# A gated recurrence followed by a SwiGLU layer on one core: integer additions moved to VectorE, gate products put ahead of the angles, loads and rows put in another order

## The chip, the cores and the metric

The kernel runs on one core of a Trainium2 chip. A core has engines that each work through their own queue of instructions in order: TensorE (PE in the profile; its weight loads are PEld), VectorE (DVE), ScalarE (ACT), GpSimd (POOL) and SyncE (SP), which here only issues DMA transfers. Engines wait for each other through semaphores. The metric is the device time of one execution in microseconds (us). Times shown are medians of several runs; the profile is of one execution.

## The reference

Two blocks follow each other. The first is a recurrence over 768 time steps for 4 x 8 heads of width 48, with a complex decay per step and feature:

```python
mag = np.sqrt(a_re * a_re + a_im * a_im)
scale = np.minimum(mag, 0.999) / (mag + 1e-06)
a_re_n, a_im_n = (a_re * scale, a_im * scale)
for t in range(S):
    new_re = ar * S_re - ai * S_im
    new_im = ar * S_im + ai * S_re
    S_re, S_im = (new_re + k v^T, new_im)
    y[t] = q[t] @ S_re
```

The second takes the 3072 rows of 384 features that come out, normalises each by its root mean square, and computes `(silu(xn @ w_gate) * (xn @ w_val)) @ w_out` with 1536 hidden features. The three weights arrive as 64-bit floats and are narrowed to 32 bits on the chip.

## The kernel before, in words

**Tiling.** The 3072 rows are 24 chunks of 128. Gates are worked out in 13 units: units 0 and 1 are one chunk each, units 2 to 12 two chunks each, so chunk 2n and 2n+1 belong to unit n+1 from chunk 2 on. Two chunks make a group of the second block (g0 to g11).

**Gates** (`gates`, L772 to L850). From re and im of a unit come, on ScalarE and VectorE in turn: the magnitude by way of reciprocal roots, cut off at 0.999; its running product p along time by a scan (L807); the angle by an arctangent (L798); its running sum by a scan (L816), reduced to a fraction of a turn (L823 and after), then a sine and a cosine (L836, L838). k is multiplied by a refined reciprocal of p, q by p, and four products with sine and cosine, ks, k, qs and q, are the "rotated" rows. ScalarE's functions lie in tables: a change of function can need a load of 1.28 us (ACT_TABLE_LOAD). A unit's first step (L772) overwrites a tile that the rotation of the unit before it reads.

**Moving rows** (`move_rows`, L861). A DMA brings the rotated rows into the tiles kr and qr, 96 partitions deep, in three transfers for each of the four. Units 0 and 1 send ks and k on SP's queue and qs and q on POOL's; the others all four on SP's. The final products `ends` go out to DRAM (dec, L873) and come back in another shape (decay, L876); SP waits for dec before it issues decay.

**Chunks.** TensorE computes for each chunk the scores s (L1014), which VectorE masks (am, L1019); it transposes k (kt, L1035), which ScalarE copies (L1039); it forms the chunk's contribution to the state (L1057); and y from both (L1087). Then come sums of squares (ss, L1110), their mean on DVE (L1115), a root on POOL (L1120), its spreading (L1123), a copy rb on ScalarE (L1128) and xT on VectorE (L615).

**Second block.** For each group, twelve gv tiles (L1160), each twelve matmul passes with a piece of w_gate and of w_val; silu on ScalarE (L1164), a product on VectorE; then four output halves (L1184), each over half of the hidden features. Three PSUM buffers hold gv tiles and outputs.

**Weights** (`fetch`, `narrow`). There are 18 pieces: 0 to 11 alternate w_gate and w_val, 12 to 17 are w_out. A raw piece of 768 KB is fetched; ScalarE turns its low words into a fraction (share, L956); VectorE shifts the high words (L961) and adds the sign (L615); GpSimd adds the two as integers (L968). The first six pieces (EARLY) are issued on POOL's queue from the start, the others on SP's after unit 0's rows. Raw buffers are shared: a later piece waits until an earlier one is narrowed.

**What sets the order.** A planner written out in Python (`Order`) holds a list of lanes, each a sequence of steps with an engine, an assumed length and needs. It repeatedly takes the step that can begin first, with an added "late" per lane, and emits its instructions, so its assumed times fix the order in each engine's queue; the actual waits come from the data. `RATE` is its assumed transfer rate, and `holds` tells it that a GpSimd addition keeps VectorE busy. `busy` (L644) emits matmuls without use, as many as fill the gap that the planner expects on TensorE, 9 us at most.

The lines that carry the rest:

```python
for i, (o, x, f) in enumerate((("ks", "k", s), ("k", "k", y), ("qs", "q", s), ("q", "q", y))):
queue = nc.gpsimd if u < 2 and i > 1 else nc.sync
nc.gpsimd.tensor_tensor(out=to, in0=part["t"], in1=to, op=ALU.add)
[("re", 0) if aside else ("moved3", 0), ("piece", before) if before is not None else None],
```

## Time and profile before

| | |
|---|---|
| median of four runs | 831.5 us (826.74 to 837.05) |
| profiled execution, whole | 829.65 us |
| its span from first to last instruction | 827.5 us |
| PE busy | 761.2 us, 92% |
| DVE busy | 430.2 us, 52% |
| ACT busy | 360.8 us, 44%; 69 table loads of 1.28 us |
| POOL busy | 79.6 us, 10% |
| granted TensorE clock, mean | 0.948 |
| TensorE matmuls without use | 28.7 us (L644) |

In the page, engine rows of 40 digits show the busy share of 40 equal slices in tenths; PEclk is the TensorE clock that the chip granted, in tenths of full speed. A row of the timeline gives start, duration, engine, line, operation, output<-inputs, shapes and a count, and in brackets the idle time before it with what ended it. A row of the waits gives who waited for whom, the total, how often, and the longest. A row of the chain gives start, duration and what the time went to, followed back from the last instruction to end; "SPq" is SyncE's queue, "DMA a<-b" a transfer in flight.

### The profile page before, as it was taken

What the parts mean: (1) busy time and instruction counts of PE and PEld (TensorE: products, weight loads), DVE (VectorE), ACT (ScalarE), POOL (GpSimd) and SP (SyncE); (2) the same over time, 40 slices, a digit from 0 to 9 for tenths busy, and PEclk for the clock granted to TensorE, in tenths of its full rate; (3) what the DMA queues carried; (4) which work ended last, traced back from release to release, by engine and by line L of the source; (5) the groups of instructions that cost most, each with busy time, mean ns of one, the idle gap of its engine ahead of it and who ended that gap; (6) DMA issues with size and microseconds to landing.
All of it is one profiled execution on the core that took longest, in us unless ns stands there. A gap on an engine that the chain in (4) does not pass through costs nothing.

```text
span 827.5 us, 12028 instructions
## 1 busy us (share of the span) xinstructions
PE 761.2 (92%) x4820; PEld 608.2 (73%) x4820; DVE 430.2 (52%) x709; ACT 360.8 (44%) x565; POOL 79.6 (10%) x103
## 2 busy tenths in 40 slices
PE   5078967989998999999999999999999999999996
PEld 2066835778886878988678888678888778886783
DVE  4666999857675775857784766122211213320220
ACT  6542475657675767767664775101111101110110
POOL 6344432200000000000010000000000000000000
PEclk9556979989998999999999999999999999999999
DMA  8929537562747267554635470046100106200510
GB/s 199 198 62 241 141 114 128 120 117 43 114 88 130 45 113 121 120 77 97 78 112 75 122 115 1 10 97 143 40 0 1 58 17 192 79 1 28 179 61 23
DMA packets 100975, 76.48 MB, mean 92 GB/s; under 512 B 39664, under 2 KB 89584, under 8 KB 100912
## 3 DMA queue, kind: packets, MB, share of 16 engines
q1 hardware_dynamic: 98128, 69.74, 39.7%
q0 software_dynamic: 1920, 5.51, 3.1%
q8 instruction: 40, 0.66, 0.4%
q10 hardware_dynamic: 864, 0.39, 0.2%
q14 instruction: 23, 0.19, 0.1%
HBM read 51.98 MB, written 4.76 MB: 69 GB/s over the span
## 4 chain that ended last, share of the span: by engine, by line
PE 74%; DMA 9%; DVE 7%; SPq 4%; ACT 2%; issue 2%; POOL 0%; DVEq 0%; ACTq 0%
PE gv_ps L1160 38%; PE out_ps L1184 20%; PE s_ps L1014 6%; PE y_ps L1087 4%; PE state_ps L1057 3%; SPq L861 3%; DMA q<-in_q_dram 3%; DMA dec<-ends 2%; PE ss_ps L1110 1%; PE kt_ps L1035 1%; DMA qr<-q 1%; DMA qr<-qs 1%; DMA vz<-in_v_dram 1%; DVE re L816 1%; DMA hT<-in_w_val_dram 1%
## 5 line engine op out<-in xcount | busy, mean ns | idle before, releaser
L1160 PE MATMUL gv_ps<-xT,wg 128*128 128x256 f32 x864 | 213.7, 384 | 0.4 <-DVE xT L615 0.3
L1160 PE MATMUL gv_ps<-xT,wv 128*128 128x256 f32 x864 | 210.3, 379 | 0.0
L1184 PE MATMUL out_ps<-wo,hT 128*128 128x384 f32 x576 | 196.6, 494 | 7.8 <-POOL wo L968 7.8
L1160 PEld LDWEIGHTS gv_ps<-xT,wg 128*128 128x128 f32 x864 | 163.2, 192 | 26.6 <-DVE xT L615 2.3
L1160 PEld LDWEIGHTS gv_ps<-xT,wv 128*128 128x128 f32 x864 | 164.6, 190 | 22.5
L1184 PEld LDWEIGHTS out_ps<-wo,hT 128*128 128x128 f32 x576 | 108.0, 192 | 76.6 <-POOL wo L968 9.6
L612 DVE TENSOR_TENSOR hT<-gv_ps,hT 128x256 f32<-128x256 f32 x144 | 59.7, 421 | 189.6 <-ACT hT L1164 189.2
L1164 ACT ACTIVATE hT<-gv_ps 128x256 f32<-128x256 f32 x144 | 54.1, 383 | 211.2 <-PE gv_ps L1160 210.7
L1014 PE MATMUL s_ps<-qr,kr 96*128 96x128 f32 x384 | 56.5, 308 | 43.2 <-DMA kr<-k 30.5
L1014 PEld LDWEIGHTS s_ps<-qr,kr 96*128 96x128 f32 x384 | 52.5, 219 | 47.3 <-issue 47.3
L1120 POOL TENSOR_TENSOR rs<-ssq,mhalf 128x1 f32<-128x1 f32 x24 | 18.5, 771 | 580.1 <-DVE ssq L1115 580.1
L1193 ACT COPY ot<-out_ps 128x384 f32<-128x384 f32 x24 | 11.5, 480 | 63.8 <-PE out_ps L1184 63.8
L615 DVE SCALAR_TENSOR_TENSOR xT<-y_ps,gcol,rb 128x128 f32<-128x128 f32 x72 | 20.8, 345 | 35.5 <-ACT rb L1128 29.6
L1019 DVE TENSOR_TENSOR am<-s_ps,causal 128x512 f32<-128x512 f32 x48 | 32.1, 684 | 11.8 <-PE s_ps L1014 11.2
L1057 PEld LDWEIGHTS state_ps<-vz,kt 128*96 128x96 f32 x320 | 31.9, 175 | 1.6 <-issue 0.5
L1164 ACT ACT_TABLE_LOAD x25 | 32.1, 1283 | 0.4
L1128 ACT COPY rb<-ss_ps 128x128 f32<-128x128 f32 x24 | 6.4, 265 | 59.4 <-PE ss_ps L1123 59.4
L1057 PE MATMUL state_ps<-vz,kt 128*96 128x48 f32 x320 | 31.9, 256 | 0.0
L1039 ACT COPY kt<-kt_ps 128x384 f32<-128x384 f32 x40 | 17.2, 478 | 25.2 <-PE kt_ps L1035 25.2
L1087 PE MATMUL y_ps<-am,vz 128*32 128x128 f32 x768 | 27.6, 287 | 0.0
L990 DVE TENSOR_REDUCE least__113<-raw 128x1 f32<-128x768 f32 x18 | 17.0, 945 | 19.3 <-DMA raw<-in_w_out_dram 16.0
L1110 PEld LDWEIGHTS ss_ps<-ones,sq 128*128 128x128 f32 x144 | 19.7, 197 | 8.5 <-ACT sq L1105 5.0
(113 smaller groups left out, 819.6 us busy)
## 6 DMA issues: line engine op xcount, KB each, us to landing
raw<-in_w_out_dram SPq DMA_DIRECT2D x12, 768.0 KB, 4.4
k<-in_k_dram SPq DMA_DIRECT2D x24, 192.0 KB, 3.1
q<-in_q_dram SPq DMA_DIRECT2D x24, 192.0 KB, 4.0
vz<-in_v_dram SPq DMA_DIRECT2D x24, 192.0 KB, 4.6
out_dram<-ot SPq DMA_DIRECT2D x24, 192.0 KB, 2.0
raw<-in_w_gate_dram SPq DMA_DIRECT2D x6, 768.0 KB, 4.6
raw<-in_w_val_dram SPq DMA_DIRECT2D x6, 768.0 KB, 4.5
re<-in_a_re_dram SPq DMA_DIRECT2D x33, 128.0 KB, 2.8
```

The costliest lines, as they stand in the source:

```text
L612: nc.vector.tensor_tensor(out=o, in0=x, in1=y, op=op)
L615: nc.vector.scalar_tensor_tensor(out=o, in0=x, scalar=c, in1=y, op0=op0, op1=op1, **kw)
L861: queue.dma_start(out=two[name][rows + j * L:rows + (j + 1) * L], in_=t[("ks", "k", "qs", "q")[i]][:, j])
L1014: nc.tensor.matmul(u["s_ps"][a][:, h], lhsT=u["k"][:, a * HH + h], rhs=u["q"][:, a * HH + h], start=True, stop=True)
L1019: nc.vector.tensor_tensor(out=u["am"][a], in0=u["s_ps"][a], op=ALU.mult, in1=causal.unsqueeze(1).to_broadcast([C, HH, C]))
L1057: nc.tensor.matmul(u["st_ps"][:, h], lhsT=u["kt"][h // HH][:, h % HH], rhs=u["v"][:, h, 0:D], start=True, stop=True)
L1087: nc.tensor.matmul(u["y_ps"][32 * p:32 * (p + 1), j], lhsT=columns(left, j, odd, p), rhs=right(h), start=side == 0 and i == 0, stop=side = ...
L1110: nc.tensor.matmul(u["ss_ps"][:, 0:1], lhsT=u["sq"][:, d], rhs=ones, start=d == 0, stop=d == ND - 1)
L1120: nc.gpsimd.tensor_tensor(out=u["rs"], in0=u["ssq"], in1=mhalf, op=ALU.pow)
L1160: nc.tensor.matmul(ps[:, i], lhsT=w_[:, f * P // FW, d, cols], rhs=t["xT"][:, d], start=d == 0, stop=d == ND - 1)
L1164: nc.scalar.activation(out=t["hT"][:, f], in_=t["gv", f][:, 0], func=AF.Silu)
L1184: nc.tensor.matmul(t["o_ps", i], lhsT=t["hT"][:, f, i * C:(i + 1) * C], rhs=wo[:, f], start=f == 0, stop=f == NF - 1)
```

## The change

It does the following, all in the fast path:

- The integer addition at the end of narrowing goes from GpSimd to VectorE; `holds` is dropped.
- In `gates`, the running product, the reciprocal root of p and the products of k and q come ahead of the angle; the range check (relu with an accumulator) comes early; the four rotations come in the order ks, qs, k, q.
- `move_rows` takes the rows in that order, so for units 0 and 1 transfers alternate between SP's and POOL's queue.
- v of unit 0 is loaded along with unit 1's; unit 2's gates are loaded after unit 1's q.
- EARLY is 3 instead of 6. Ahead of these pieces POOL copies one column of unit 1's k, so that they begin once that has landed. The other pieces start after unit 1's rows.
- w_out pieces may be narrowed later (WO); the planner's rate is 0.22 for all queues together.
- The matmuls without use ahead of chunk 0's scores are seven that read unit 0's ks.

```diff
-    RATE = 0.2
+    RATE = 0.22
...
-            for n in range(first_, first_ + m):
+            for n in range(0 if u == 1 else first_, first_ + m) if u else ():
...
-                more["late"] = lambda: 0.1 if ("piece", 11) in order.ends else 0.6
+                more["late"] = lambda: 0.1 if ("piece", 11) in order.ends else 0.3
...
+            check = E("ACT", 0.2 + ac_us(n1), [], lambda: act_(out=qs, in_=qs, func=AF.Relu, bias=width,
+                                                               accum_out=range_[:, u:u + 1]), K("checked"))
...
-            yield E("DVE", tt_us(n1), [K("y0")], lambda: tt(im, im, y), K("t0"))
...
-            yield E("DVE", tt_us(n1), [K("abs")], lambda: tt(re, re, y))
...
             yield E("DVE", 0.4 + n1 / 480, [], products, K("p"))
 
+            yield E("DVE", tt_us(n1), [K("y0")], lambda: tt(im, im, y), K("t0"))
+            yield E("DVE", tt_us(n1), [K("abs")], lambda: tt(re, re, y))
+            yield E("DVE", tt_us(n1), [], lambda: stt(im, re, 2.0, im, ALU.subtract, reverse0=True), K("tan"))
+            yield E("ACT", ac_us(n1), [K("p")], lambda: act_(out=r, in_=p, func=AF.Abs_reciprocal_sqrt),
+                    table=["ars"])
+            yield E("ACT", ac_us(n1), [], lambda: act_(out=r, in_=r, func=AF.Square), K("r2"))
+            yield E("ACT", ac_us(n1), [K("tan")], lambda: act_(out=im, in_=im, func=AF.Arctan), table=["atan"])
+            yield E("ACT", ac_us(n1), [], lambda: act_(out=im, in_=im, func=AF.Copy, scale=0.5 / PI), K("turns"))
+            yield E("DVE", tt_us(n1), [K("r2")], lambda: tt(ks, p, r))
+            yield E("DVE", tt_us(n1), [], lambda: stt(r, ks, 2.0, r, ALU.subtract, reverse0=True))
+            yield E("DVE", tt_us(n1), [K("k")], lambda t=t: tt(t["k"], t["k"], t["r"]))
+            yield E("DVE", tt_us(n1), [K("q")], lambda t=t: tt(t["q"], t["q"], t["p"]))
...
-            for i, (o, x, f) in enumerate((("ks", "k", s), ("k", "k", y), ("qs", "q", s), ("q", "q", y))):
+            for i, (o, x, f) in enumerate((("ks", "k", s), ("qs", "q", s), ("k", "k", y), ("q", "q", y))):
...
-                queue = nc.gpsimd if u < 2 and i > 1 else nc.sync
+                queue = nc.gpsimd if u < ASIDE and i % 2 else nc.sync
...
-    EARLY = 6
+    EARLY = 3
...
+        yield step("POOL", 0.2, [("k", 1)],
+                   lambda: nc.gpsimd.tensor_copy(out=behind, in_=UN[1]["k"][:, 0, 0:1]), ends=["rows in"])
...
-                       [("re", 0) if aside else ("moved3", 0), ("piece", before) if before is not None else None],
+                       ["rows in" if aside else ("moved1", 1), ("piece", before) if before is not None else None],
...
             def total(to=to.bitcast(I32), part=part):
-                nc.gpsimd.tensor_tensor(out=to, in0=part["t"], in1=to, op=ALU.add)
+                tt(to, part["t"], to, ALU.add)
...
-            yield step("POOL", 2.3, [("both", i)], total, ends=[("piece", i)], holds=("DVE", 1.2))
+            yield step("DVE", tt_us(n), [], total, ends=[("piece", i)], **more)
...
-                    if a == 0:
+                    if a == 0 and n:
                         busy(flat(u["s_ps"][a]))
+                    elif a == 0:
+                        rotated = flat(UN[0]["ks"])
+                        for _ in range(7):
+                            nc.tensor.matmul(flat(u["s_ps"][a])[:, 0:ND * C], lhsT=ident, rhs=rotated,
+                                             start=True, stop=True)
```

## The prediction

> **What bounds the kernel now.** I read the page's busy table and slices first, then the chain that ended last, then the waits, then the timeline of the first 270 us.
>
> ```profile
> PE 761.2 (92%) x4820; PEld 608.2 (73%) x4820; DVE 430.2 (52%) x709; ACT 360.8 (44%) x565; POOL 79.6 (10%) x103
> PE   5078967989998999999999999999999999999996
> PEclk9556979989998999999999999999999999999999
> ...
> PE s_ps L1014 <- DMA kr<-k: 30.5, 2, 29.9
> ...
> 17.53 20.71 DMA q<-in_q_dram
> 38.26 6.37 DMA dec<-ends
> ...
> 131.73 5.65 DMA dec<-ends
> ...
> 168.65 6.88 DMA qr<-q
> ...
> 251.71 7.48 DMA dec<-ends
> 259.27 3.75 PE s_ps L1014 x16
> ```
>
> TensorE bounds the whole from slice 12 on. What can be won lies in the first third: slices 1 to 12, where it waits or runs at a low clock (5, 5, 6 and 7 tenths in slices 1, 2, 3 and 5; each is 20.7 us).
>
> To add up such a stretch I use a **lag**: clock time minus the full-speed TensorE work that stands ahead in its queue. Full-speed prices are from chain rows that run warm: scores of a chunk 1.85 us, turned keys 0.7, state 1.32, each half of y 0.95, ss 0.85, a gv tile (12 matmuls) 2.59, half an output row block 3.88. The whole kernel is 706.2. The first scores of chunks 0, 2, 4, 6, 8 and 10 start at 44.2, 137.5, 175.7, 221.5, 259.3 and 302.8 with 0, 47.3, 79.9, 119.6, 152.6 and 193.0 ahead. The lags are 44.2, 90.2, 95.8, 101.9, 106.7 and 109.8. TensorE's last output matmul ends at 820.5: lag 114.3. So 110 of 114 us are lost by chunk 10, and only that stretch can pay. 7.0 us of closing work follow, the same in both.
>
> **Part by part.** I take the changed kernel's built order of instructions on each engine and put durations of this trace on it.
>
> Start to the first scores. Before, six weight pieces go out on POOL's queue from 5.5 us, and unit 1's k row, issued at 12.25, reaches its consumer at 36.1 (23.8 us at the longest). Changed, k, q and v of unit 1 stand on SP ahead of unit 2's gates (issue done by about 8.8 by the same 0.6 us rows; unit 2's gates, 2 us later so, are read only at 40), POOL waits for that k (about 10: 1.3 MB at the 199 GB/s of slice 0), and only three pieces follow (piece 0 in at about 20, since piece 0 took 5.5 to 14.5 before). That is an added wait on two engines: behind POOL's stand only the pieces and unit 0's q rows. ScalarE has piece 0's share between unit 0's angle and unit 1's roots; by 0.44 us steps and one 1.28 table load it gets there at 19.9, so they meet. Each us that piece 0 is later costs one us of all that follows. Four loads of 1.28 stand ahead of unit 0's sine (three before). The rotation of unit 0 ends at 30.5 (28.3 before), a loss of 2.2; that of unit 1 at 37.1 (41.1 before). Then the rows: before, the queues are full, SP's first three issues take 6.28, and scores start at 44.2, 16 us after the rotation. After unit 1 the same step took 1.86 + 1.85 of issues and 2.30 of landing. Changed: in by about 36. Seven warm-up matmuls behind ks take 14 half passes, 9 at the cold 0.64 and 5 at 0.32: until 36.6. First scores **36.6, gain 7.6**. The ten warm-ups at 2.65 to 14.3 that this drops hid nothing.
>
> To the first gv tile. SP still waits twice for dec (6.4 and 4.2 us from issue to decay) and issues gcol (3.29); piece 3, early before, stands behind both: issued at 52.4 to 55.2, in at 58 to 59. VectorE has its shift ahead of chunk 1's mask, ScalarE its share ahead of chunk 1's turned keys and chunk 0's rb. So chunk 1 waits for piece 3: the wait that takes the place of the old ones. From 58.5, DVE: mask, xT, mask, 0.95 + 1.0 for piece 3, five gate operations, scan 1.76, mean at 69, rs, rb, three gate operations, xT at 73. First gv **73.3 against 77.6**, but cold, because five of the six warm-ups ahead of gv are gone: 2.7 lost. Twelve tiles end at about 107 (108.5). Pieces 4 to 11, 3.1 us apart as pieces 6 and 7 were before (74.46 and 77.59), keep half a us ahead of it.
>
> The additions. POOL's 18 take 1.81 to 2.46 us, and DVE does not run beside them:
>
> ```profile
> 82.77 1.82 POOL L968 TENSOR_TENSOR wv<-t,wv 128x768 int32<-128x768 int32 x1 [1.37 <-DVE wv L615]
> 82.94 2.06 DVE L961 TENSOR_SCALAR t<-raw 128x768 int32<-128x768 int32 x1
> 92.34 0.55 DVE L961 TENSOR_SCALAR t<-hT 128x768 int32<-128x768 int32 x1
> 119.25 2.46 DVE L612 TENSOR_TENSOR k<-k,r 128x768 f32<-128x768 f32 x1
> 121.63 0.95 DVE L612 TENSOR_TENSOR q<-q,p 128x768 f32<-128x768 f32 x1
> ```
>
> The same shift takes 2.06 beside POOL and 0.55 alone; some 15 DVE operations are stretched by about 1.5, 23 us in all. The new form is built as an instruction over 128x1536 halves, and no row shows it. Bounds: 0.55 (one-source int32 pass) and 1.84 (twice a two-source pass); below nothing is excluded, the elements must be read. I take 0.95, the nearest row: the same bytes, two sources. 18 x 0.95 = 17 against 23: DVE gains 6, and each piece is ready about 1 us sooner. At 1.84 it is 33, DVE loses 10, and 7 of them lie ahead of gv's last pieces and unit 2.
>
> The Trainium skill (VectorE: DVE Perf Modes, Mode 2x_1P) lets unit-stride 16-bit operands of a two-input operation run two per cycle at 0.96 GHz, which as an estimate makes 0.8 us and a fixed part; by it the sum moves by under 3 us. No run here shows that mode.
>
> Unit 2. Its rotation ended at 126.4 because of the held DVE and the wo pieces (TensorE stood 4.99 us for wo at 110 to 115). Changed, behind piece 11 (100.1): products 2.8, sums 2.0, round, fraction, abs, two sines without a load, four rotations: 111.6. Rows 12 us later, as before (126.4 to 137.5, last q row 5.8 after its issue), so chunk 2 at **123**, with 43.4 ahead: lag **79.6 (90.2)**. But three output halves and the fourth (15.5 us), done by 164 before, are now undone; WO keeps them for later gaps. Next, xT of chunk 3 hangs on ScalarE: piece 14's share waits for a transfer behind dec of unit 2 (in at 129.4), then turned keys, atan, sq. gv of group 1 starts at 144.8, cold (2.7). Unit 3 rotates until 149.6, so chunk 4 at **162.5**, 70.9 ahead: lag **91.6 (95.8)**.
>
> From here TensorE has the kept halves to work on. Chunk 6: 43.5 us of work later, 206; unit 4 rotated at 193 + 12 = 205. No stall: lag **91.5 (101.9)**. Unit 5 at 225 + 12 = 237, wanted at 234: 2.7 waited. A row prices such a wait: at 175.67, 2.21 idle is followed by scores in 3.75 and gv slowed, 3.3 lost. Lag after it 97.6 (109.1). Unit 6 at 263 + 12 = 275, wanted at 273: 2.1 and half a re-warming: **101.4 (109.8)**. Chunk 12 has 50 us of work ahead: dense. To the end the old run adds 4.5: 105.9 against 114.3.
>
> The skill (TensorE: Matmul & The Clock Gate, What's actually happening) speaks of a re-throttle only after an idle window of about 3.4 us; by it those two waits would cost 5 less. The row at 175.67 shows a slow pass after 2.21, so the row decides.
>
> Edits at nothing: fewer table loads (69 to 61, 10 us off an engine at 44%; the change does not bring two a unit everywhere); range check moved forward, hidden by DVE's scan; the q rows stay on POOL for units 0 and 1, merely interleaved; RATE and late act only through the order, counted above.
>
> **Sum:** 105.9 - 114.3 = -8.4. The profiled execution was 829.65 (span 827.5 and 2.15 around it), which would be 821.2; the median shown is 831.5, so **823**.
>
> **Rivals.** The forecast is (A). (E) The waits at chunks 8 and 10 do not come and piece 3 lands 3 sooner: kept halves speak for it; 9 us more: 814. (B) The additions cost 1.84, or piece 0 comes 7 late through three transfers on a busy queue (before, quarters took 4.8 to 9): +7: 830. For it: the built form has 1536 elements. Against: DVE loses 23 of stretch. (C) Slower: the angles now stand behind the products. Two operations, copies and the scan (4.1 us) come ahead of each arctangent; 2.85 of products and a load leave the end of the chain. Units hang on each other (ACT s waits for DVE qs nine times, 30.2 us), so if that credit fails, units 3 to 6 come 4.1 later each: 16.4 at chunk 10 and a re-warming of 3.3: -8.4 + 19.7 = +11: 843. It decides from 2.1 us more spacing than the 38 I counted; the old spacing was 37 to 45. (D) The early gain is real but hidden: TensorE's queue has the same late units ahead, lag 109 at chunk 10: 831.
>
> **How the numbers follow.** One per cent (8.3 us) is about what a measurement of this kernel tells from no change. Chances: 0.34 for 823 (half of it beyond 1%), 0.27 for E, 0.18 for B and D together, 0.21 for C. Faster by over 1%: 0.44; within: 0.35; slower: 0.21. The range takes all of A, B and D, E with 6 us of further luck, and C up to its middle, which leaves out about 0.14: 808 to 842. The likeliest case alone: 816 to 829.
>
> **What would show it.** Right: unit 1's k in by 11; first scores at 35 to 38; DVE idle for piece 3 until 58; no DVE operation of 768 over 1.1; the addition at 0.9 to 1.0; chunk 2 at 120 to 126; lag at chunk 6 about 92. Wrong: scores after 42 (piece 0 held ScalarE), additions at 1.8, rotations over 40 apart.

## The result and the profile after

The changed kernel takes 837.5 us at the median (834.0 to 847.4, 38 runs), the kernel before, beside it, 833.7 (59 runs). The ratio is 1.0056, 95% interval 1.0038 to 1.0074: **slower by 0.56%**, some 5 us, where 823 was forecast. The ratio leaves out the executions that ran over 1.5% above the fastest of their kernel, so it is not quite that of the two medians. The time lies inside the range, in the part that was kept for rival C; the sign is wrong.

The profiled execution of the changed kernel took 841.1 us (span 839.2), 3.6 above its median; that of the kernel before lay 4.0 below its own. The two traces are therefore 11.4 us apart where the medians are 3.8 apart. Part of such a difference is TensorE's clock: among the changed kernel's runs the time goes with the mean granted clock, from 834.0 us at 0.968 to 844.3 at 0.953, and the profiled one had 0.956. The last section shows one stretch that does this; what is read below from this one trace stands under that reserve.

The page of the changed kernel, its busy table and two of its rows of 40 slices (21.0 us each):

```profile
PE 759.5 (91%) x4816; PEld 611.1 (73%) x4816; DVE 426.7 (51%) x727; ACT 350.1 (42%) x557; POOL 37.2 (4%) x74
...
PE   0368968879989989999999999999999999999996
...
PEclk9976985899989999999999999999999999999998
```

POOL's work has halved and ScalarE lost 11 us, as it should. TensorE still bounds the whole, and what it loses still lies in the first third. Counted from 0, slices 5 to 8 are busy by 6, 8, 8 and 7 tenths, much as before (6, 7, 9, 8), but the clock in slice 6 is at half, where it was at nine tenths.

Its waits, TensorE's costliest (what waited, for what, us in total, times, longest):

```profile
PE s_ps L1020 <- DVE ks L608: 29.7, 1, 29.7
PE s_ps L1023 <- DMA dec<-ends: 17.3, 4, 10.3
PE ss_ps L1119 <- ACT sq L1114: 6.0, 5, 3.1
PE kt_ps L1044 <- ACT rb L1137: 5.9, 1, 5.9
PE ss_ps L1132 <- POOL rs L1129: 5.2, 3, 2.2
```

The first is the wait from the start to the warm-ups. The second is the wait of late chunks for a unit's rows (four times, 17.3 us; before, rows put down to the decay or to q made 11.0 in three). It goes under the name of the transfer issued last behind them, dec<-ends, which the scores don't need: chunk 2's scores began at 128.9, and that store landed only at 130.3. The fourth is chunk 1's wait for piece 3, whose share stands on ScalarE ahead of rb. The two of ss are longer than before (3.3 and 1.4): with nothing else in the queue, TensorE stands through the small steps between a chunk's y and its gv tiles.

The chain that ended last (start, us, what), only the pieces that matter:

```profile
121.58 7.03 DMA dec<-ends
...
128.90 3.75 PE s_ps L1023 x16
...
167.22 9.31 DMA dec<-ends
...
177.94 6.93 DMA raw<-in_w_out_dram
...
215.81 7.64 DMA dec<-ends
...
289.25 7.92 DMA dec<-ends
```

Unit after unit the chain goes through the landing of a unit's rows (again under the name dec<-ends), and after unit 3's through a piece of wo, which the chain of before doesn't do in this stretch.

In the prediction's own measure, the lag (clock time minus TensorE work written ahead), at the scores of each chunk:

```
chunk              0     2     4     6     8     10    end
before            44.2  90.2  95.8 101.9 106.7 109.8 114.3
forecast          36.6  79.6  91.6  91.5  97.6 101.4 105.9
after             41.8  85.5 104.0 109.3 117.3 121.9 125.8
```

5 us are won by chunk 2, half of what was forecast. Then 18.5 are lost up to chunk 4 (5.6 before), 5.3, 8.0 and 4.6 up to the next ones.

What TensorE did between the scores of chunk 2 and the gv tiles of group 1 shows the difference. First the timeline of the kernel before (start, us, engine, line, operation):

```profile
151.54 4.12 PE L1184 MATMUL out_ps<-wo,hT 128*128 128x384 f32 x12
...
155.72 4.04 PE L1184 MATMUL out_ps<-wo,hT 128*128 128x384 f32 x12
...
160.18 4.12 PE L1184 MATMUL out_ps<-wo,hT 128*128 128x384 f32 x12
...
165.42 1.56 PE L1160 MATMUL gv_ps<-xT,wg 128*128 128x256 f32 x6
```

and the same place in the changed kernel:

```profile
137.19 2.69 PE L1066 MATMUL state_ps<-vz,kt 128*96 128x48 f32 x16
...
144.69 1.56 PE L1066 MATMUL state_ps<-vz,kt 128*96 128x48 f32 x16
...
150.73 0.49 PE L1132 MATMUL ss_ps<-ident,rs 128*128 128x128 f32 x2 [1.84 <-POOL rs L1129]
151.97 1.44 PE L1119 MATMUL ss_ps<-ones,sq 128*128 128x1 f32 x6 [0.75 <-ACT sq L1114]
154.60 0.80 PE L1132 MATMUL ss_ps<-ident,rs 128*128 128x128 f32 x2 [1.19 <-POOL rs L1129]
...
156.90 2.17 PE L1169 MATMUL gv_ps<-xT,wg 128*128 128x256 f32 x6
```

Before, three output halves of group 0 run warm while ScalarE, POOL and VectorE take a chunk from y to xT. Changed, there is nothing but the small matmuls themselves, and the state sums take 2.69 instead of 1.48: the clock is at half. Both kernels need about the same time from chunk 2's scores to that gv tile (27.9 us before, 28.0 changed), but before, 11.6 us of it are output halves.

ScalarE at the same time, on the chain of unit 3's gates (line 811 is the root of the product, 814 the arctangent, 959 a share of a wo piece, 1048 the copy of turned keys):

```profile
133.33 0.48 ACT L1048 COPY kt<-kt_ps 128x384 f32<-128x384 f32 x1 [7.89 <-PE kt_ps L1044]
...
136.02 0.90 ACT L959 ACTIVATE wo<-raw 128x768 f32<-128x768 uint32 x1 [1.57 <-DMA raw<-in_w_out_dram]
136.83 0.82 ACT L811 ACTIVATE r<-p 128x768 f32<-128x768 f32 x1
...
140.58 0.48 ACT L1048 COPY kt<-kt_ps 128x384 f32<-128x384 f32 x1 [2.05 <-PE kt_ps L1044]
...
143.01 0.84 ACT L814 ACTIVATE im<-im 128x768 f32<-128x768 f32 x1
```

Unit 3's products were ready at 127.7, but its root stands behind chunk 2's keys and a piece of wo, and its arctangent behind chunk 3's. Before, the arctangent ran at 138.9, 1.4 us after chunk 2's scores had begun, and no key copy stood ahead of it:

```profile
138.91 0.84 ACT L798 ACTIVATE im<-im 128x768 f32<-128x768 f32 x1 [0.64 <-DVE im L615]
139.78 0.84 ACT L799 ACTIVATE im<-im 128x768 f32<-128x768 f32 x1
141.46 0.90 ACT L1039 COPY kt<-kt_ps 128x384 f32<-128x384 f32 x2 [0.84 <-PE kt_ps L1035]
```

From unit 2's row issue to unit 3's 46.0 us pass (113.25 to 159.26), 37.4 before.

### The profile page after: what moved, and what is told of

It reads as the page before. It is cut to its first block, busy times and chain, and to the rows that moved or that the text cites. A ratio compares the mean times of both kernels' runs of the same rounds, so it can differ in the third digit from the quotient of the medians.

```text
span 839.2 us, 12004 instructions
## 1 busy us (share of the span) xinstructions
PE 759.5 (91%) x4816; PEld 611.1 (73%) x4816; DVE 426.7 (51%) x727; ACT 350.1 (42%) x557; POOL 37.2 (4%) x74
## 4 chain that ended last, share of the span: by engine, by line
PE 73%; DMA 9%; DVE 8%; ACT 4%; SPq 3%; issue 2%; POOL 0%; DVEq 0%; ACTq 0%
PE gv_ps L1169 39%; PE out_ps L1193 18%; PE s_ps L1023 5%; DMA dec<-ends 4%; PE y_ps L1096 4%; PE state_ps L1066 3%; PE kt_ps L1044 2%; PE ss_ps L1119 1%; SPq L862 1%; DMA qr<-qs 1%; DVE re L826 1%; DVE q L608 1%; DMA raw<-in_w_out_dram 1%; DVE w L611 1%; DVE p L802 1%
## 5 line engine op out<-in xcount | busy, mean ns | idle before, releaser
L1193 PE MATMUL out_ps<-wo,hT 128*128 128x384 f32 x576 | 194.2, 492 | 0.0
L1169 PEld LDWEIGHTS gv_ps<-xT,wv 128*128 128x128 f32 x864 | 164.8, 191 | 22.6
L1023 PE MATMUL s_ps<-qr,kr 96*128 96x128 f32 x384 | 56.2, 307 | 24.0 <-DMA dec<-ends 17.3
L1202 ACT COPY ot<-out_ps 128x384 f32<-128x384 f32 x24 | 11.4, 477 | 88.6 <-PE out_ps L1193 88.5
L1020 PE MATMUL s_ps<-ks,ident 128*128 128x384 f32 x14 | 7.6, 721 | 29.7 <-DVE ks L608 29.7
L1020 PEld LDWEIGHTS s_ps<-ks,ident 128*128 128x128 f32 x14 | 4.0, 291 | 32.7 <-issue 32.3
```

The costliest lines, as they stand in the source:

```text
L1023: nc.tensor.matmul(u["s_ps"][a][:, h], lhsT=u["k"][:, a * HH + h], rhs=u["q"][:, a * HH + h], start=True, stop=True)
L1169: nc.tensor.matmul(ps[:, i], lhsT=w_[:, f * P // FW, d, cols], rhs=t["xT"][:, d], start=d == 0, stop=d == ND - 1)
L1193: nc.tensor.matmul(t["o_ps", i], lhsT=t["hT"][:, f, i * C:(i + 1) * C], rhs=wo[:, f], start=f == 0, stop=f == NF - 1)
```

## The theories and the experiments

**Theory 1, angles.** The new order of the gates puts a unit's angles behind its products, and so behind the chunk that is just arriving; units come further apart (rival C of the prediction).

**Theory W, the kept halves.** WO = 2 takes the output halves away from the wait where they ran, and nothing replaces them.

**Theory 2, later theory P, the plan.** The order in all queues is written from assumed times. Read off while the planner writes its order, its clock for the scores of chunks 2, 4, 6, 8 and 10, beside the trace:

```
                        c2      c4      c6      c8     c10
before, plan          121.2   157.6   198.8   233.2   274.6
before, late by        16.3    18.1    22.7    26.1    28.2
after, plan           110.3   146.3   191.9   221.2   256.1
after, late by         18.6    28.6    31.8    38.8    41.1
```

The plan thinks the changed kernel 18.5 us ahead at chunk 10, the run has it 5.6 ahead there, with 17.7 less work done. Two of the plan's prices are far off in the trace. It moves a unit's rows, 1.57 MB in 4 x 3 transfers, at 0.22 MB per us (7.3 us); the DMA rate while they move is 105 to 130 GB/s, so 12 to 13. And it counts 1.3 us of SP for the decay, where SP stands until the products' ends have gone out (timeline of SP, changed kernel):

```profile
121.58 0.56 SPq L874 DMA_DIRECT2D dec<-ends  x1
130.27 0.81 SPq L877 DMA_DIRECT2D decay<-dec  x2
```

8.7 us pass between the two, and the next unit's loads and the wo pieces are queued behind.

**Theory 3, SP.** This wait, not the order, keeps the units apart.

Times below are medians; ratios are to the kernel before, measured beside each run.

### One part undone

`e1_old_gates`: the hunk of `gates` reversed (arctangent, sums and fraction ahead of the roots again), all else as changed.

```diff
-            yield E("DVE", 0.4 + n1 / 480, [], products, K("p"))
             yield E("DVE", tt_us(n1), [K("y0")], lambda: tt(im, im, y), K("t0"))
...
             yield E("ACT", ac_us(n1), [K("tan")], lambda: act_(out=im, in_=im, func=AF.Arctan), table=["atan"])
+            yield E("DVE", 0.4 + n1 / 480, [], products, K("p"))
```

> The changed kernel with one part undone: a unit's angles stand ahead of its products again, as before the change (the new order of the rotations and of the rows stays). Changed kernel 837.5, before 833.7. Theory 1 (angles): in the changed kernel's trace unit 3's roots and its arctangent stand on ScalarE behind the key copies of chunks 2 and 3 and a share of wo, and four VectorE operations stand ahead of its sums, so unit 3's rotation ends 46 us after unit 2's. Undone, units 3 to 6 come 38 to 40 apart, chunk 4 starts before 170, and the time falls by 8 to 14: 824 to 830. Theory 2 (order of TensorE's queue): what counts is how much work the written order puts ahead of a chunk. This version puts less there than the changed one (97.6 against 114.4 at chunk 6, 167.6 against 175.3 at chunk 10), so TensorE waits as much or more: 837 to 845. Theory 3 (SP): a unit's rows take 12 us on SP and the decay's round trip 7 to 9 more before the next unit's loads; the gates' order does nothing: 836 to 839.

843.1, ratio 1.013 (1.005 to 1.022). The first scores come at 34.8 instead of 41.8. The units do come closer (40.0 us from unit 2 to 3, chunk 4 at 166.2), as theory 1 says, and the time rises all the same, as theory 2 says: lag 100.5 at chunk 4 and 114.8 at chunk 6. The written order has 31.9 us of work between chunks 4 and 6, which started 46.2 apart.

`e2_add_only`: the kernel before, with the new addition alone, planned as a step of VectorE.

```diff
-                nc.gpsimd.tensor_tensor(out=to, in0=part["t"], in1=to, op=ALU.add)
+                tt(to, part["t"], to, ALU.add)
```

> The kernel before with one part of the change alone: the narrowing's last addition on VectorE instead of POOL (with the planner's note that POOL holds VectorE dropped). By the prediction VectorE gains 6 us before unit 2 and no more than that can reach TensorE: 828 to 833 against 833.7. If the additions are what costs (their 0.95 us stands on VectorE where POOL's did not): 835 to 840. If POOL's additions were hidden anyway: 833 to 834. No VectorE operation over 768 elements should be stretched over 1.1 us.

828.9, ratio 0.998 (0.994 to 1.002). In its trace the lag is 86.4 at chunk 2 and 110.2 at chunk 22, 4 less than before at either, but 100.6 at chunk 4 and 105.4 at chunk 6, 5 and 3.5 more; by the interval it is no more than the same.

`e3_old_start`: six early pieces, fetched as before; values and unit 2's gates in their old places.

```diff
-    EARLY = 3
+    EARLY = 6
-        yield step("POOL", 0.2, [("k", 1)],
-                   lambda: nc.gpsimd.tensor_copy(out=behind, in_=UN[1]["k"][:, 0, 0:1]), ends=["rows in"])
```

> The changed kernel with the start undone: six pieces on POOL's queue from the start again, no wait of POOL for unit 1's k row, values and unit 2's gates in the old places; all else stays. Chunk 0 should start at 44 instead of 41.8. If the early gain of the changed kernel is real and carried to the end, this is slower by the 2 to 5 us: 840 to 843. If it is hidden behind the late units (theory 1 or 2): 836 to 838. If the changed start itself costs, because chunk 1 waits for piece 3 (in at 61): faster, 830 to 834.

875.5, ratio 1.051 (1.044 to 1.058): far beyond any theory. Chunk 0 starts at 46.5 instead of 41.8, but of the 33 us of lag that it has more at the end only 6 are there at chunk 2; 21 come up between chunks 14 and 18, where no scores wait. One part undone changes the whole written order, so this run doesn't price the start.

`e4_dec_first`: the decay's round trip ahead of the row transfers on SP.

```diff
+            yield step("SP", 1.3, [("p", u)], decays, mb=0.02, then=2.5, ends=[("rows", u)])
             for i in range(4):
                 aside = u < ASIDE and i % 2
...
-            yield step("SP", 1.3, [("p", u)], decays, mb=0.02, then=2.5, ends=[("rows", u)])
```

> The changed kernel with the decay's round trip ahead of a unit's four row transfers in SP's program, instead of behind them: it needs the products alone, which the change puts first. Theory 3 (SP): from unit 2 on the round trip (8.7 us from issue to decay at unit 2, 9.3 at unit 3) no longer stands between a unit's rows and the next unit's loads; the loads are issued 7 to 9 us earlier and units come 4 or more us closer: 815 to 828. Theory 1 (angles): unit 3's chain hangs on ScalarE and VectorE behind chunks 2 and 3, not on its loads, so 834 to 838; only the out rows and wo pieces behind the decay come earlier. The scores after a unit's rows should start 0 to 2 us sooner, since the rows' own 1.57 MB at 120 GB/s take most of the 12 us.

846.9, ratio 1.016 (1.009 to 1.022). The loads behind the rows of units 2 and 3 do go out earlier (at 120.3 and 164.8, not 131.7 and 178.4), yet the rows of units 2, 3 and 4 are 44.9 and 46.2 apart (46.0 and 47.2 in the changed kernel). Theory 3 as it stood falls. The lag is 6 lower at chunk 6 and 5 higher at the end.

### The lateness of wo, SP's wait, and the prices

`e5_wo_only`:

```diff
-    WO = 2
+    WO = 0.3
```

> The changed kernel with one number put back: the pieces of wo are narrowed with 0.3 us of lateness, as before, not with 2 (which holds them back until chunk 3's part of the second group stands). Theory W (the kept output halves): in the changed kernel TensorE has nothing between the scores of chunks 2 and 3 (128.9 to 137) and group 1's gate matmuls (156.9) but small cold work, where the kernel before ran three output halves warm (151.5 to 164); its lag grows by 18.5 from chunk 2 to chunk 4, against 5.6. With wo early, 32.6 us of work stand between them, as before: lag at chunk 4 below 97, time 826 to 831. Theory 1 (angles): the units still come 46 us apart, so the work moved forward is missing later, at chunks 6 and 8: 835 to 838, lag over 118 at chunk 10.

843.3, ratio 1.011 (1.005 to 1.017). The first half of theory W came out: lag 94.9 at chunk 4. But chunk 6 then waits 5.7 us, the lag is 114.0 at chunk 8 and 117.8 at chunk 10: what the halves filled first is missing next, as the rival had it. Putting the halves back doesn't win the time back.

`e6_split_decay`: from unit 2 on, store and read back are two steps of the plan.

```diff
-            yield step("SP", 1.3, [("p", u)], decays, mb=0.02, then=2.5, ends=[("rows", u)])
+            if u >= 2:
+                yield step("SP", 0.6, [("p", u)], store, mb=0.02, then=6.0, ends=[("dec", u)])
+            yield step("SP", 1.3 if u < 2 else 0.9, [("p", u) if u < 2 else ("dec", u)], decays, mb=0.02, then=2.5,
+                       ends=[("rows", u)])
```

> The changed kernel with the decay of units 2 on made of two steps of the plan: the store of the products' ends, and the read back, which the planner may now put later, so that SP doesn't stand 7 to 9 us between them but issues wo pieces and the next unit's loads. Theory P (SP's blind wait: the plan counts 1.3 us for a step in which SP stood 8.7): loads of unit 4 go out at about 170 instead of 178, units come 4 to 8 closer, chunk 8 starts before 253; 822 to 832. Theory W: units earlier by some us do not help while the second group's wait is empty; the written order has even less work ahead of chunk 4 (64.4 against 70.9): 834 to 842.

838.9, ratio 1.005 (1.001 to 1.008). The units now come much sooner: the rows of units 3, 4, 5 and 6 go out at 146.3, 188.3, 227.2 and 262.6, up to 19 us ahead of the changed kernel, and the time is the same. That is the clearest sign that late units are not all that binds: the written order has as little work ahead of them (64.4 at chunk 4), and the masks of chunks 2 and 3 now stand behind unit 3's gates (8.0 us of wait in chunk 3's scores).

`e7_priced`: the two prices set to the trace, no instruction added or removed.

```diff
-                           lambda i=i, move=move: move(i), mb=0.2 * m,
+                           lambda i=i, move=move, u=u: move(i), mb=0.2 * m * (1.7 if u > 1 else 1.0),
-            yield step("SP", 1.3, [("p", u)], decays, mb=0.02, then=2.5, ends=[("rows", u)])
+            yield step("SP", 1.3 if u < 2 else 9.0, [("p", u)], decays, mb=0.02, then=2.5, ends=[("rows", u)])
```

> The changed kernel with the planner's prices for units 2 on set to what the trace shows: row transfers 1.7 times as long (1.57 MB take 12 to 13 us), and a decay that holds SP for 9 us. No instruction is added or taken out; the order alone is another. Theory P (the plan): the plan has chunk 2 at 110 and chunk 4 at 146, the run had 129 and 175; with true prices more work stands ahead of the late chunks (76.0 at chunk 4, 150.0 at chunk 8, 190.9 at chunk 10, against 70.9, 142.7 and 175.3) and less time is lost at them: lag at chunk 10 112 to 117, time 828 to 833. Theory 1 (angles): the order around the chunks is not the point, the chain of a unit is; 836 to 840.

824.5, ratio 0.985 (0.979 to 0.991): 13 us faster than the changed kernel by the order alone, more than theory P asked for. In its trace no scores wait from chunk 4 on but for 0.5 us at chunk 9, although units 4 to 6 come within 5 us of where they came in the changed kernel (281.7 against 281.4 for unit 6). This trace is of the slowest of its four runs, 831.9.

`e8_old_gates_wo`: the edits of e1 and e5 together.

> Both undone at once: the angles ahead of the products again, and wo's lateness 0.3. Against the run with wo's lateness alone this shows what the gates' order is worth when TensorE has its fill. Theory 1 (angles): 6 or more us faster than that run. Theory W: within 4 us of it, since units 40 or 46 apart make no difference while 58.8 us of TensorE's work belong to each two chunks; the written order puts only 65.7 ahead of chunk 4 here, so rather slower than that run: 830 to 836.

843.1, ratio 1.009 (1.006 to 1.013): the same as e5 within 0.2. With the old prices, the gates' order is worth nothing here.

### What fitting prices show of the parts

`e9_before_priced`: the prices of e7 in the kernel before.

> The kernel before, with the planner's two prices of the run that priced them as measured (rows of units 2 on 1.7 times as long, a decay that holds SP 9 us), and no part of the change. If the fitting prices are worth the same without the change (the plan of the kernel before was 16 us early at chunk 2 and 28 at chunk 10): lag at chunk 10 near 103, since 209.9 us of work stand ahead of it instead of 193.0; 820 to 828. If it is the change that made the plan unfit (its plan is 19 early at chunk 2 and 41 at chunk 10) and the kernel before fitted well enough: 831 to 836. The three pieces of wo that stay on time here speak for little change after chunk 4.

821.3, ratio 0.983 (0.976 to 0.990). So the plan of the kernel before was unfit as well, and by about as much. The lag stays at 99.8 to 102.5 from chunk 4 to chunk 16. This takes away half of theory P: the old prices hold 13 us of the changed kernel, but they hold as much of the other.

`e10_old_gates_priced`: e7 with the gates' old order.

> The changed kernel with the fitting prices, and the angles ahead of the products as before: the same as the priced run but for the gates' order. Theory 1 (angles): units come 40 instead of 46 us apart and now the order leaves TensorE work, so 4 to 10 us faster than the priced run (824.5): 814 to 821. Theory P (the plan alone): the gates' order is not felt, or is worse, because this order once more puts less work ahead (145.9 at chunk 8, 183.1 at chunk 10, against 150.0 and 190.9): 824 to 834.

817.1, ratio 0.976 (0.969 to 0.983). Units 2 and 3 are 37.7 apart (45.8 in e7, but 40.7 in e17, the same program), chunk 0 starts at 36.7 (42.9).

`e11_store_early`: new gates, the rows' price, and the ends stored ahead of the rows (as soon as the products are there) and read back as a step behind them; scores need only the rows.

```diff
+            if u > 1:
+                yield step("SP", 0.6, [("p", u)], store, mb=0.02, then=1.5, ends=[("dec", u)])
             for i in range(4):
...
+            yield step("SP", 1.3 if u < 2 else 0.9, [("p", u) if u < 2 else ("dec", u)], decays, mb=0.02, then=2.5,
+                       ends=[("rows", u)])
```

> The changed kernel with the rows' price as measured and, from unit 2 on, the products' ends stored ahead of the row transfers and read back as a step of its own behind them, so that SP waits for no round trip; the plan lets the scores go with the rows, without the decay. More work is written ahead of the late chunks than in the priced run (160.4 at chunk 8, 202.1 at chunk 10) and a unit's loads go out 7 to 9 us earlier. Theory P: lag at chunk 10 98 to 106, time 812 to 822. If the 4-byte elements of the store hold the rows up behind them on the queue, chunk 2 comes 3 or more later and 822 to 828.

823.5, ratio 0.985 (0.978 to 0.993): no better than e7. Lag 102.4 at chunk 10, in the range said, but another 3 are lost at chunk 16.

`e12_rows_priced`: the first line of e7's edit alone.

> The changed kernel with the rows' price alone (1.7 times as long from unit 2 on), the decay at its old 1.3 us. Of the two prices this one moves more work ahead of the chunks (160.4 at chunk 8 and 204.7 at chunk 10, against 150.0 and 190.9 with both). If the rows' landing is the plan's main error: 820 to 828, as with both. If it is SP's stand for the decay: 833 to 838.

832.6, ratio 0.995 (0.991 to 1.000). Between the two answers: about half of e7's gain. The decay's price carries the other half.

`e13_gates_only_priced`: the kernel before, fitting prices, and the new gates' order alone.

> The kernel before with the fitting prices and one part of the change: the products ahead of the angles. Against the same without it (821.3). Theory 1 (angles): unit 3's rotation comes 44 to 47 us after unit 2's instead of 38, and the lag at chunk 6 is 5 or more higher: 826 to 832. If the difference of 7 us between the two priced versions of the changed kernel comes from how the orders happened to fall, not from the chain: 818 to 823.

836.0, ratio 1.001 (0.996 to 1.006) against 0.983 without it. Units 2 and 3 are 44.4 apart (37.9 in e9). Of the 15 us only 3.4 are there at chunk 10; 11 more are lost in one stretch at chunks 16 to 18.

`e14_add_priced`: the kernel before, fitting prices, and the addition on VectorE.

> The kernel before with the fitting prices and the integer addition on VectorE alone. Against 821.3 without it. The prediction's term (VectorE gains 6 us by piece 11 and unit 2): unit 2's rotation 8 us sooner than 129.4 and lag at chunk 4 5 less: 814 to 819. If POOL's additions and the held VectorE were hidden: 820 to 823. The additions at 0.95 us.

843.7, ratio 1.012 (1.004 to 1.020): a miss for both answers. At chunk 8 the lag is 2.3 lower than in e9 (98.9), but then 12 us go between chunks 10 and 12 and 12.5 between chunks 16 and 18, each around one gap of TensorE (6.8 and 9.1 us) with slow matmuls behind it. The second gap, on TensorE and then on ScalarE:

```profile
458.33 1.46 PE L1160 MATMUL gv_ps<-xT,wv 128*128 128x256 f32 x6
468.88 2.93 PE L1160 MATMUL gv_ps<-xT,wg 128*128 128x256 f32 x6 [9.09 <-DVE hT L612]
```

```profile
454.64 0.48 ACT L1193 COPY ot<-out_ps 128x384 f32<-128x384 f32 x1 [8.96 <-PE out_ps L1184]
455.02 0.94 ACT L785 ACTIVATE qs<-re,mid 128x768 f32<-128x768 f32 x1
...
465.82 0.84 ACT L835 ACTIVATE w<-im 128x768 f32<-128x768 f32 x1 [0.29 <-DVE im L615]
466.69 1.28 ACT L1164 ACT_TABLE_LOAD   x1
467.98 0.66 ACT L1164 ACTIVATE hT<-gv_ps 128x256 f32<-128x256 f32 x2
```

Thirteen us of a unit's gates stand ahead of the silu that frees TensorE's buffers: ScalarE waited 8.96 for an output and took up the gates that the order has behind it. A written order can lose time in the dense part too.

`e15_old_start_priced`: e10 with the start undone (the edit of e3).

> The fastest run so far (changed kernel, old gates' order, fitting prices: 817.1) with the start undone: six pieces on POOL's queue, no wait for unit 1's k row. Chunk 0 should start at 44 to 46 instead of 36.7. If the gain at the start is carried on (prediction: 7.6 us at the first scores): 823 to 828, lag at chunk 2 91 against 84.7. If the weight pieces, not the first scores, set group 0's start: the same lag at chunk 2 and 815 to 819.

824.0, ratio 0.988 (0.981 to 0.996) against 817.1. Chunk 0 at 46.1 instead of 36.7; lag 89.5 against 84.7 at chunk 2, 104.2 against 96.2 at chunk 4, 107.9 against 102.6 at chunk 23. This is what the prediction said of the start, carried to the end: 5 us of lag in these traces, 7 us of time (10 by the ratio of e10, 6 by that of the same program in e18, with intervals that overlap).

`e16_store_early_old_gates`: e11 with the old gates' order.

> The changed kernel with the old gates' order, the rows' price, and the products' ends stored ahead of the rows and read back later. Theory 1 with theory P: the gates' order is worth 4 to 8 here too against the same with the new order (823.5): 812 to 820. If the two do not add, since TensorE no longer waits for a unit after chunk 2 in either: 819 to 824.

813.9, ratio 0.973 (0.965 to 0.982): the fastest median, ahead of both kernels and 10 below e11, though its interval overlaps those of e10 and e11. Here units 2 and 3 are 45.5 apart in spite of the old order: unit 3's arctangent has slipped behind chunk 2's masks. So it isn't the gates' order as such that spaces them, but on which side of an arriving chunk the angle ends up, and TensorE, with 151.3 us written ahead of chunk 8, hardly feels it. e6 is the counterpart: with the new order, unit 3's arctangent ran at 135.7, ahead of chunk 2's key copies (146.0), and units 2 and 3 are 34.1 apart.

`e17_new_gates_again` and `e18_old_gates_again`: e7's and e10's kernels once more, side by side on one chip.

> The changed kernel with both fitting prices (rows 1.7 times as long, a decay that holds SP 9 us), the new gates' order; beside the next run on one chip, to measure the gates' order directly. From the first run of this order: ratio to the kernel before 0.985 and 45.8 us between the rotations of units 2 and 3. Theory 1: at least 5 us above the next run.

> The same with the angles ahead of the products. Theory 1 (the gates' order costs by itself): ratio 0.972 to 0.980, 37.6 us between the rotations of units 2 and 3. If the 7 us were the spread of runs: within 3 us of the run beside it.

822.8, ratio 0.988 (0.984 to 0.992), and 818.2, ratio 0.981 (0.978 to 0.984). With fitting prices the gates' order costs 4.7 us by the medians, just under what theory 1 asked for, 6 by the ratios; the intervals don't touch. Units 2 and 3 are 40.7 and 37.7 apart. The spacing isn't all of it: the first scores come at 43.1 and 34.9, and of the 7.5 us between the two traces' lags at the end (107.5 and 100.0) 2.6 are there at chunk 2. With the old order, ScalarE's arctangent of unit 3 falls into the wait for chunk 2's rows (its scores begin at 127.5):

```profile
125.15 0.84 ACT L795 ACTIVATE im<-im 128x768 f32<-128x768 f32 x1 [1.30 <-DVE im L611]
126.03 0.84 ACT L796 ACTIVATE im<-im 128x768 f32<-128x768 f32 x1
131.93 0.86 ACT L1046 COPY kt<-kt_ps 128x384 f32<-128x384 f32 x2 [5.05 <-PE kt_ps L1042]
```

In e18 it runs at 125.2, in a time when ScalarE has nothing else; in e17 it ran at 140.7, in the changed kernel at 143.0.

In e17, chunks 2, 4, 6, 8 and 10 come 14.7, 15.5, 16.8, 16.2 and 16.0 us after the plan: late from the start on, but hardly later as it goes, where the changed kernel's lateness grew from 18.6 to 41.1.

## Why the prediction was wrong

**The start.** Right: unit 1's k at POOL by 9.7 (said 10), piece 0 at 20.0, the rotations of units 0 and 1 at 30.9 and 37.2 (30.5 and 37.1), the warm-ups. Wrong: the first scores at 41.8 instead of 36.6. The step "in by about 36" failed: the rows needed 11 us from the rotation. The last to land was the third transfer of unit 0's own k, issued on SP at 33.0 and landed at 41.6 (view of the tile kr from 29 to 36 us; the last line is the time from issue to landing of the transfers of ks and k together):

```profile
L862 SPq DMA_DIRECT2D kr<-k x3: 609/613/691, 31.6 to 33.0; - x3
...
DMA to landing us min/median/max: 2.7/5.3/8.7
```

The chain names a transfer of unit 1 on POOL's queue (issued at 38.3), which chunk 0 doesn't read and which landed after its scores had begun. A second part is the new order of the gates: with the angles first again, unit 0's rotation ends at 26.7 instead of 30.9 and the first scores come at 34.8 (e1; 34.5 to 36.7 in e8, e10, e16 and e18). The prediction saw 2.2 us of loss at that rotation, but no more behind it. The gain of the rest of the new start was of the right size and kept to the end, 7 us, once the prices fitted (e15, with the old gates).

**To chunk 2.** gv started at 76.1 (said 73.3), unit 2's rotation ended at 115.8 (111.6), chunk 2 came at 128.9 (123), after 13.1 instead of 12 us of rows (the row that the prediction names, 126.4 to 137.5, shows 11.1). 5.9 of the 19.9 us by which the lag at the end was missed are made here. SP stood 8.5 us for unit 0's decay, where the prediction had up to 6.4, and piece 3, which it rightly saw behind both decays and ahead of chunk 1, was in at 61 instead of 58 to 59.

**The additions.** Right in their price: 18 times 0.95 to 0.96 us. VectorE is 3.5 us less busy in all (6 said), and no 768-wide operation but the scans (1.76) is over 0.96, where some had been at 1.9 to 2.6 and one at 5.3.

```profile
L608 DVE CUSTOM_DVE_ANT_0 wg<-t,wg 128x1536 uint16<-128x1536 uint16 x6 | 5.7, 955 | 0.1
```

(a group: busy, mean ns, idle before it). The Trainium skill (VectorE: DVE Perf Modes, Mode 2×_1P) would have 1536 16-bit elements at two per cycle in an estimated 0.8 us and a fixed part; the measured 0.955 leaves 0.15 for that part, so the run agrees. What the additions bring could not be separated: less lag at chunk 2 in two traces (3.9 in e2, 9.8 in e14), but more at chunks 4 and 6 in e2 and 2.3 less at chunk 8 in e14, then no measurable time in e2 and a loss through later gaps in e14.

**Unit 3, the step that failed first.** "Unit 3 rotates until 149.6" took 38 us from unit 2 to 3, the spacing of the old order. It was 46.0, and the rotation ended at 161.8. Rival C named this term, the angles behind the products, and priced it at 4.1 us a unit, "from 2.1 us more spacing"; it came at unit 3 with 8.6 more than before and at unit 4 with 2.7 more, and not at units 5 and 6. Two things are in the 46.0. One is the order: not the operations that were put ahead of each arctangent (they are 4 us) but the arriving chunk that these push the arctangent behind. The other is the clock after chunk 2's wait, which the prediction had only as 2.7 us of cold gv matmuls: the one program of e7 and e17 has 45.8 us where TensorE stayed at half clock for 15 us, as in the changed kernel's trace, and 40.7 where it did for 4.6. Against e18 (37.7, also short) the order's own share of the spacing is 3.0 us there; in e13 against e9, both short, it is 6.5 (44.4 and 37.9). Direct measure of the order with fitting prices: 4.7 us of time (e17 against e18). With the old prices, undoing the order didn't win the time back (e1).

**Between chunk 2 and group 1, the step that failed next.** The prediction has 21.8 us from chunk 2 (123) to the first gv tile of group 1 (144.8); the changed kernel's trace has 28.0. So 12.0 us of lag were counted up to chunk 4 and 18.5 were lost. TensorE's order in this stretch is the same in e7 and e17, which took 27.9 and 22.6 (129.5 to 157.4, and the rows of e17):

```profile
130.18 3.75 PE L1023 MATMUL s_ps<-qr,kr 96*128 96x128 f32 x16 [10.29 <-DMA dec<-ends]
...
152.82 2.57 PE L1169 MATMUL gv_ps<-xT,wg 128*128 128x256 f32 x6
```

With the short half clock the count was nearly right. No output half fills the stretch, as the prediction knew; what it had wrong is the price of that emptiness, matmuls at half clock that hold up the chain of unit 3. 6.5 of the miss at the end are made here. Another 5.4 come up to chunk 6, said to come without a stall: the kept halves do stand ahead of its scores (four of them, from 210.7 to 222.5), and TensorE waited only 1.2 us there, but unit 4 rotated 48.2 us after unit 3, where 43.4 had been taken, and the wait of 2.9 us at chunk 4 was followed by 3.3 of slow scores and 1.8 of waiting for the copies of its keys.

**The waits at chunks 8 and 10.** 2.7 and 2.1 us were said, 1.2 and 2.9 stood; but 8.0 and 4.6 of lag came up towards them, where 6.1 and 3.8 were said. The scores took 2.0 us after the wait of 1.2 and 2.8 after that of 2.9, against 1.85 warm.

**What remains.** With fitting prices the changed kernel stands at 0.985 (e7) and 0.988 (e17) of the kernel before, and the kernel before at 0.983 (e9). The intervals overlap (0.984 to 0.992 for e17, 0.976 to 0.990 for e9), so these runs don't show whether the half per cent is still there. The old prices made both slower by 12 to 15 us, so they are not shown to set the two apart either. What is shown with fitting prices is a start that gains some 7 us (e15) and an order of the gates that costs some 5 (e17 against e18; 15 in the kernel before, e13, of which 11 in one stretch of the dense part). These two alone don't add up to a kernel that is 5 us slower. The additions, WO and the rows on two queues were not separated, since each single edit moves the whole order and single gaps of 10 us with it, and one execution's clock can move a trace by 4 us or more. That the gaps in the dense part come from gates standing ahead of a silu was read from one trace, not tried. So the steps of the prediction that failed are known, but the cause of the sign stays open.

## What to carry to other kernels

Where a planner fixes the order of in-order queues, compare its clock with the trace before any other change: two wrong prices were worth 1.7 to 2.1% in either kernel, and until they fitted, undoing one part or adding one gave ratios from 0.998 to 1.051. Fitting prices don't make single edits additive either: one part added to the kernel before still cost 15 and 22 us (e13, e14), most of it in single gaps far from the edit. Before reading a spacing from one trace, compare the granted clock there with another execution of the same program. Look at what an arriving piece of work pushes a chain behind, not at how many operations were put ahead of it. Look up in the built order what fills the bound engine's next wait, and price the stretch at the low clock if nothing does.

## What was not expected of the hardware

**TensorE's clock after a wait.** e7 and e17 are one program. Both start chunk 2's scores after 10.2 and 10.3 us of idle (129.5 and 130.2), at half clock, and then run on almost without a gap. In windows of 5 us (the window's length, then the busy time of PE, PEld, DVE, ACT and POOL with their instructions, then the granted clock, the DMA engines' busy share and GB/s), first e7, then e17:

```profile
130.00:135.00 5.00, 5.00 (x28) 5.00 (x27) 2.43 (x4) 0.94 (x3) 0.00 (x0) 0.50 0.24 67
135.00:140.00 5.00, 5.00 (x29) 5.00 (x28) 2.07 (x3) 1.61 (x3) 0.00 (x0) 0.50 0.86 241
140.00:145.00 5.00, 5.00 (x75) 4.42 (x74) 1.98 (x3) 3.08 (x4) 0.00 (x0) 0.50 1.08 282
```

```profile
130.00:135.00 5.00, 4.82 (x26) 4.85 (x27) 1.72 (x3) 0.39 (x1) 0.00 (x0) 0.54 0.11 30
135.00:140.00 5.00, 5.00 (x88) 4.89 (x91) 4.42 (x7) 3.56 (x7) 0.00 (x0) 1.00 0.74 215
```

In e17 the clock is full after 4.6 us of work; in e7 it stays at 0.50 for 15 us of work without a pause. On VectorE the masks and states of this stretch stand between unit 3's steps, and its rows went out 4.5 us later (159.7 against 155.2 us). The lag is 4.1 us apart at chunk 4 (101.4 against 97.3) and 6.1 at chunk 6; the whole executions took 831.9 and 822.6, so some 3 us came later. The changed kernel's own trace is of the long kind (0.50 from 125 to 140, 0.53 to 145), that of the kernel before of the short one (0.81 from 135 to 140 with scores from 137.5, 0.85 to 145, then 1.00), which is a part of why the two traces are further apart than the medians. Why one execution stays at half clock and another doesn't is not shown. The Trainium skill (TensorE: Matmul & The Clock Gate, What's actually happening) has a window of about 3.4 us that runs freely, so that the number of slow matmuls varies from run to run; the run-to-run difference agrees, the length doesn't: 15 us at half clock are more than four such windows of busy time, so here the measurement stands.

**The products' ends.** The store of 3 KB took 8.7 us from issue to landing behind a unit's rows on the queue (unit 2, changed kernel), and 4.3 ahead of them (e4, unit 3: 133.4 to 137.7).
